# Moving a fetch into the middle of GpSimd's solve, and early parts between stages, in an RWKV-7 and FFN kernel

## The chip, the cores and the metric

The kernel runs on one core of a Trainium2 chip. A core has five engines that run side by side, each with its own queue of instructions taken in order: TensorE (PE, matmuls; its weight loads are listed as PEld), VectorE (DVE), ScalarE (ACT), GpSimd (POOL) and SyncE (SP). They meet through semaphores. Transfers run on 16 DMA engines; SP and GpSimd issue them here, and a transfer that has to wait for something holds up all that stands behind it on the queue that issues it. The metric is the device time of one execution in microseconds (us).

## The reference

First an RWKV-7 recurrence, for 4 batches of 8 heads, 768 steps, head dimension 40. All of it is 32-bit floating point.

```python
for t in range(S):
    kt, vt, rt = (k[:, :, t], v[:, :, t], r[:, :, t])
    wt, at, bt = (w[:, :, t], a[:, :, t], b[:, :, t])
    y[:, :, t] = np.einsum('bhd,bhde->bhe', rt, state)
    Sa = np.einsum('bhde,bhe->bhd', state, at)
    state_decay = state * wt[:, :, None, :] - np.einsum('bhd,bhe->bhde', Sa, bt)
    state = state_decay + np.einsum('bhd,bhe->bhde', vt, kt)
```

Then y, laid out as 3072 tokens of 320 channels, goes through a feed-forward net with a squared ReLU:

```python
h = np.maximum(x @ w_in, 0.0)        # w_in: 320 x 2048
return (h * h @ w_out)               # w_out: 2048 x 320
```

The two weights come as 64-bit numbers and are turned into 32-bit ones by the kernel itself.

## The kernel before

**Chunks.** A recurrence step by step would be 768 steps long, so the sequence is cut into 6 chunks of 128 steps for each of 4 batches: 24 chunks, in the order chunk 0 of every batch, chunk 1 of every batch, and so on. A chunk takes all 8 heads. Within it the recurrence becomes matrix products, with one thing left that is sequential: a strictly triangular 128 x 128 matrix for each head (N, the products of b and a under the decays) must be turned into the inverse of a unit triangular matrix, called T here. T is found for two 64 x 64 halves of each head, and the block between the halves is applied by a product.

**The parts of a chunk.** Each is a Python generator that emits a few instructions to several engines and then yields.

- `early(i)` (L341): loads of w, b and a; transposes of w on TensorE; running products of the decays on VectorE (L351, L352); their two reciprocals (L355, L356); transposes of b and a; bT and aT (L359, L360); the products N on TensorE, copied out by ScalarE (L367 to L372). The decays are stored in HBM (kept_e) for later, and N in blocks (kept_q for the first six chunks, kept_d after them, kept_n for the part between the halves).
- The inverse: `take(u)` (L403, its transfer L412) fetches N of a whole unit of chunks into the tile half_n, one (chunk, head, half) to a partition or two, and `solve(u)` (L414) runs the forward substitution on GpSimd, row by row: at each step s one product (L435) and one subtraction (L437), then the result half_t is stored as kept_t (L440). It is written over by the next unit, whose memset (L425) waits for the store.
- `inverses(i)` (L444): T of one chunk is loaded from kept_t, by SP (L451). For the first six chunks GpSimd has only inverted 32 x 32 blocks (L457 loads them); two rounds of small products, the joins, make the 64 x 64 inverses of them (emitted at L479 and L487, `mm` at L87 is the line that the profile shows).
- `rest(i)` (L494): loads of k, r, v, b (L142) and of the kept decays (L152); the products A, RV; T.
- `chain(i)` (L561): what depends on the state of the chunk before: xr and its products with T, the new state, RX, and the output tokens.
- `ffn()` (L655): for each three chunks of finished tokens, w_in products (ps_f from tokens), squares on VectorE, w_out products.
- `rounding()` (L249): the weights' conversion, in pieces, by ScalarE and VectorE, in stages 0 to 4.

**Units.** GpSimd solves chunks in units: unit 0 holds chunk 0, unit 1 chunk 1, unit 2 chunks 2 and 3, unit 3 chunks 4 and 5, unit 4 chunks 6 and 7, unit 5 chunks 8 and 9, unit 6 chunks 10 to 13, unit 7 chunks 14 to 17, unit 8 chunks 18 to 21, unit 9 chunks 22 and 23. Units 0 to 3 are the fine ones (32 x 32 blocks, 31 steps); the others have 63 steps.

**Stages.** After a prelude (chunks 0 to 3's early parts and units 0 to 2), the main loop has 24 stages, one for each chunk i. A stage weaves, step by step over 12 steps, the chain of chunk i, some steps of `ffn`, the `rest` of chunk i + 1, the early parts of the chunks in `ahead[i]`, and in the first stages pieces of the weights. Nothing reorders what is emitted: each engine runs its queue as the weave wrote it. After each stage, where all chunks of the next unit have had their early parts, the loop emits its fetch and its solve:

```python
ahead = {0: (4, 5), 1: (6, 7), 2: (8,), 3: (9,), 4: (10, 11), 5: (12, 13)}
ahead.update({i: (i + 8,) for i in range(6, len(order) - 8)})
...
while unit < len(units) and all(m_ in done for m_ in range(len(order)) if unit_of[m_] == unit):
    flush()
    take(unit, own)
    solve(unit)
    unit += 1
```

GpSimd has nothing else to do in the main loop, so it runs fetch, solve, store, fetch, solve, store as fast as the chunks' blocks come, far ahead of or behind the stage in which these were emitted. SP's queue holds, in the order of the weave, the loads of `rest` and `early`, the stores of N and the decays, the moves of finished tokens (L108), and the loads of T, each of which waits for its unit's store.

Of the kernel before, what the change touches and what calls it, by code (L numbers as in the profile page):

```python
# [17 lines left out]
def kernel(  # L18
# [22 lines left out]
    nc = tc.nc  # L41
    ctx.enter_context(tc.manual_schedule())
    B, H, S, D = r.shape
    DM = H * D
    DFF = moe_w_in.shape[1]
    C = 128
    MID = C // 2
    HC = C // 2
# [67 lines left out]
    class Ring:  # L116
# [6 lines left out]
        def next(self):  # L123
            self.at = (self.at + 1) % len(self.tiles)
            return self.tiles[self.at]
# [173 lines left out]
    FINE = 4  # L299
# [41 lines left out]
    def early(i, g=None):  # L341

        x_ = early_loaded.pop(i)
        dec = decays.next() if g is None else kept_here[i]
        if g is not None:
            nc.vector.memset(dec[:, :A_, :, MID:MID + 1], 1.0)
        up, down, aT = (dec[:, n] for n in (UP, DOWN, A_))
        wT = turn(x_["w"])
        yield
        for q in range(NP):  # L350
            nc.vector.tensor_tensor_scan(up[:, q, MID + 1:C + 1], wT[:, q, MID:], ones, 1.0, Alu.mult, Alu.mult)  # L351
            nc.vector.tensor_tensor_scan(down[:, q, MID - 1::-1], wT[:, q, MID - 1::-1], ones, 1.0, Alu.mult, Alu.mult)  # L352
        yield
        bT_, aT_ = turn(x_["b"]), turn(x_["a"])
        nc.vector.reciprocal(down[:, :, MID + 1:C + 1], up[:, :, MID + 1:C + 1])  # L355
        nc.vector.reciprocal(up[:, :, :MID], down[:, :, :MID])  # L356
        yield
        bT = turned("bT", 1)
        nc.vector.tensor_tensor(bT, bT_, down[:, :, 1:C + 1], Alu.mult)  # L359
        nc.vector.tensor_tensor(aT[:, :, :C], aT_, up[:, :, :C], Alu.mult)  # L360
        if g is None:
            store(kept_e[i], dec[:USED])
        yield
        bb, c = order[i]
        t_ = new("N", [128, H, C], 1)
        even, odd = products(bT, aT[:, :, :C])
        nc.scalar.copy(t_[:, :NP], even)  # L367

        for half in range(2):
            own_, other = (slice(n * HC, (n + 1) * HC) for n in (half, 1 - half))  # L370
            nc.scalar.copy(t_[own_, NP:, own_], odd[other, :, other])
        nc.scalar.copy(t_[:HC, NP:, HC:], odd[:HC, :, HC:])  # L372
        joins = lambda half: t_[half * HC:half * HC + Q, :, half * HC + Q:(half + 1) * HC]
        for half in range(2):
            for n in range(2):
                at = half * HC + n * Q
                if i < SMALL:
                    kept, to = kept_q[i, :, half, n], at + Q
                else:
                    u = unit_of[i]  # L380
                    kept, to = kept_d[u][i - units[u][0], :, half], (half + 1) * HC
                    kept = kept[:, n * Q * HC:n * Q * HC + Q * (to - at)].rearrange("h (s t) -> h s t", s=Q)
                store(kept.rearrange("h s t -> s h t"), t_[at:at + Q, :, at:to], 1, nc.scalar if g is not None and n else nc.sync)
            if i < SMALL and g is None:
                store(kept_m[i][half], joins(half), 1)
        if g is None:
            store(kept_n[i], t_[:HC, :, HC:], 1)
        else:
            g["dec"], g["N"] = dec, new("N21", [HC, H, HC], 2)
            nc.scalar.copy(g["N"], t_[:HC, :, HC:])  # L390
            g["joins"] = spare("joins", i)
            for half in range(2):
                nc.scalar.copy(g["joins"][half * HC:half * HC + Q], joins(half))
        yield
# [5 lines left out]

    part_of = lambda u: given[:, u % 3 * Q * Q:(u % 3 + 1) * Q * Q] if u < FINE else given

    def take(u, queues):  # L403
        first, nb = units[u]
        if u < FINE:
            kept = kept_q[first:first + nb].rearrange("b h f k s t -> (b h f k) (s t)")
        else:
            kept = kept_d[u].rearrange("b h f w -> (b h f) w")
        cols = classes(u)
        rows = 128 // cols  # L410
        for col in range(cols):
            queues[col % len(queues)].dma_start(out=part_of(u)[col * rows:(col + 1) * rows], in_=kept)  # L412

    def solve(u, between={}):  # L414

        first, nb = units[u]
        fine = u < FINE
        size = Q if fine else HC
        cols = classes(u)
        rows = 128 // cols  # L420
        part = part_of(u)
        words = size // cols * size
        at = u * Q * Q // 2 if fine else 0
        ts = solved[:, at:at + words]
        nc.gpsimd.memset(ts, 0.0)  # L425
        for col in range(cols):
            nc.gpsimd.memset(ts[col * rows:(col + 1) * rows, col::size + cols], -1.0)
        t3 = ts.rearrange("p (j t) -> p j t", t=size)
        for s in range(size - 1):
            if s in between:  # L430
                between[s]()
            n, m_ = s // cols + 1, size - 1 - s
            at = s * size + s + 1 if s < Q else Q * HC + (s - Q) * (Q + 1) + 1
            p_ = new("half_p", [128, 528], 1)[:, :n * m_].rearrange("p (j t) -> p j t", j=n)
            nc.gpsimd.tensor_tensor(p_, part[:, at:at + m_].unsqueeze(1).to_broadcast([128, n, m_]),  # L435
                                    t3[:, :n, s:s + 1].to_broadcast([128, n, m_]), Alu.mult)
            nc.gpsimd.tensor_tensor(t3[:, :n, s + 1:], t3[:, :n, s + 1:], p_, Alu.subtract)  # L437
        to = kept_t[u]
        to = to.rearrange("n b h f k j t -> (n b h f k) (j t)") if fine else to.rearrange("n b h f j t -> (n b h f) (j t)")
        nc.gpsimd.dma_start(out=to, in_=ts)  # L440
# [3 lines left out]
    def inverses(i, g, queue=nc.sync):  # L444
        bb, c = order[i]
        u = unit_of[i]
        kept = kept_t[u][:, i - units[u][0]]
        g["T"] = T = new("T", [128, H, HC], 2)
        if u >= FINE:
            for col in range(classes(u)):  # L450
                queue.dma_start(out=T[col::classes(u)], in_=kept[col].rearrange("h f j t -> (f j) h t"))  # L451
        else:


            blocks = new("blocks", [128, H, Q], 1)
            for col in range(classes(u)):
                queue.dma_start(out=blocks[col::classes(u)], in_=kept[col].rearrange("h f k j t -> (f k j) h t"))  # L457
        if "N" not in g:
            g["N"] = new("N21", [HC, H, HC], 2)
            queue.dma_start(out=g["N"], in_=kept_n[i])  # L460
            if u < FINE:
                g["joins"] = spare("joins", i)
                for half in range(2):
                    queue.dma_start(out=g["joins"][half * HC:half * HC + Q], in_=kept_m[i][half])
        if u >= FINE:
            return
        yield
        upper_ = spare("turned", i)
        nc.vector.transpose(upper_.rearrange("p h t -> p (h t)"), blocks.rearrange("p h t -> p (h t)"))
        for n in range(2):  # L470
            nc.scalar.activation(T[:, :, n * Q:(n + 1) * Q], blocks, Act.Copy, scale=which[:, n:n + 1])
        yield
        small = lambda: psum(ps_w)[:, :H * Q].rearrange("p (h t) -> p h t", h=H)
        p_ = small()
        mv = spare("mv", i)
        ends_ = [(slice(half * HC, half * HC + Q), slice(half * HC + Q, (half + 1) * HC)) for half in range(2)]
        for one, two in ends_:
            for h in range(H):
                mm(p_[two, h], g["joins"][one, h], upper_[one, h], True)  # L479
        for one, two in ends_:  # L480
            nc.scalar.copy(mv[two], p_[two])
        yield
        p_ = small()
        for one, two in ends_:
            for h in range(H):
                mm(p_[one, h], mv[two, h], blocks[two, h], True)
        for one, two in ends_:  # L487
            nc.scalar.copy(T[one, :, Q:], p_[one])
        yield
# [205 lines left out]
    def run(gen):  # L695
        for _ in gen:
            tick()
# [87 lines left out]


    TOTAL = 12
    ahead = {0: (4, 5), 1: (6, 7), 2: (8,), 3: (9,), 4: (10, 11), 5: (12, 13)}
    ahead.update({i: (i + 8,) for i in range(6, len(order) - 8)})

    PER, LAG = NF // 2 + 4 * GB, 3
    by_then = [0] * B + [5]
# [3 lines left out]
    pieces_in = {0: (4, TOTAL), 1: (6, TOTAL), 2: (6, TOTAL), 3: (7, TOTAL), B: (4, 4)}  # L796
    done = set(range(B))
    unit = unit_of[B]
    for i in range(len(order)):
        bb, c = order[i]  # L800
        n, begin = share[i]
# [16 lines left out]
        weave(*jobs)  # L818
        while unit < len(units) and all(m_ in done for m_ in range(len(order)) if unit_of[m_] == unit):
            flush()  # L820
            take(unit, own)
            solve(unit)
            unit += 1
    flush()
    run(second)
# [30 lines left out]
```

## Time and profile before

| | |
|---|---|
| median of 11 runs | 1063.18 us (1061.2 to 1066.32) |
| the profiled execution's own time | 1064.23 us |
| its span | 1062.5 us |
| TensorE busy | 943.4 us, 89% of the span |
| GpSimd busy | 667.1 us, 63% |
| VectorE busy | 497.6 us, 47% |
| ScalarE busy | 273.1 us, 26% |
| granted TensorE clock, mean | 0.90 of full |
| GpSimd idle before L435, for fetched blocks (kept_d) | 59.5 us in 6 waits |
| GpSimd idle before L412, for a unit's blocks to be stored | 36.2 us in 3 waits |
| TensorE idle for T | 16.6 us in 2 waits |

Where GpSimd stood with each unit, in us from the start of the span:

| unit | chunks | fetch issued | first product | result's store issued |
|---|---|---|---|---|
| 3 | 4, 5 | 111.37 | 122.21 | 149.55 |
| 4 | 6, 7 | 157.37 | 173.80 | 250.76 |
| 5 | 8, 9 | 251.36 | 265.81 | 345.23 |
| 6 | 10 to 13 | 346.00 | 356.85 | 478.21 |
| 7 | 14 to 17 | 489.16 | 505.47 | 627.30 |
| 8 | 18 to 21 | 646.52 | 662.98 | 783.88 |
| 9 | 22, 23 | 784.58 | 797.99 | 878.64 |

The stages' first products (A with v) start at 104.43 us for stage 1, 154.28 for stage 2, then 192.76, 231.67, 279.94, 321.77, 356.39, 398.93, 435.57, 469.82 for stage 10, 526.17, 561.95, 597.80, 641.60 for stage 14, 683.21, 720.44, 759.82, 791.16 for stage 18, 835.94, 873.85, 903.85, 935.09 and 971.86 for stage 23.

In a line of the profile's timeline the first number is the start in us, the second the length in us, then engine, line of the kernel, operation, what is written and read, and how many instructions were merged (x16 and the like). A bracket gives the idle time of the engine just before, and what is taken to have ended it: the last event on record, which need not be the true one. A q behind an engine's name is its queue of DMA and semaphore instructions. The row PEclk of the page shows TensorE's granted clock in tenths of full speed.

### The profile page before, as it was taken

How to read it: one execution, taken by the hardware profiler on the slowest of the kernel's cores; microseconds unless marked ns; L12 is line 12 of the kernel's file. 1: busy time of each engine (PE TensorE's matmuls, PEld its weight loads, DVE VectorE, ACT ScalarE, POOL GpSimd, SP SyncE). 2: the span in 40 equal slices, each digit the busy share in tenths (PEclk: the TensorE clock that was granted, in tenths of full speed). 3: DMA queues.
4: the chain of work that ended last, by engine and by line, in shares of the span. 5: the costliest groups of instructions: out<-in, count | busy, mean ns of one | idle time of the engine just before them, and what ended most of it. 6: DMA issues, size and time to landing. Idle time of an engine off the chain costs nothing.

```text
span 1062.5 us, 19797 instructions
## 1 busy us (share of the span) xinstructions
PE 943.4 (89%) x7824; PEld 683.8 (64%) x7824; DVE 497.6 (47%) x940; ACT 273.1 (26%) x627; POOL 667.1 (63%) x1124
## 2 busy tenths in 40 slices
PE   6364668779999999997999998999997999999998
PEld 5264556667677766774677666776675677757656
DVE  5456786697564375251663453363522442222120
ACT  3132332443322223221212222213211222232020
POOL 4778464885888699981899951999958980000000
PEclk8656565578999999998999999899998999999999
DMA  8988989759647916528647618544344431430000
GB/s 106 152 142 147 177 194 176 146 128 181 102 78 140 191 44 93 110 44 177 108 59 135 112 63 140 87 101 77 50 113 95 65 48 53 98 45 7 22 1 19
DMA packets 260168, 106.92 MB, mean 101 GB/s; under 512 B 243660, under 2 KB 249292, under 8 KB 258412
## 3 DMA queue, kind: packets, MB, share of 16 engines
q1 hardware_dynamic: 255740, 86.65, 46.7%
q0 software_dynamic: 3248, 18.88, 7.9%
q8 instruction: 62, 1.02, 0.4%
q10 hardware_dynamic: 1088, 0.13, 0.1%
q14 instruction: 30, 0.25, 0.1%
HBM read 72.47 MB, written 31.19 MB: 98 GB/s over the span
## 4 chain that ended last, share of the span: by engine, by line
PE 56%; POOL 20%; DMA 11%; DVE 5%; issue 4%; ACT 3%; SPq 2%; DVEq 0%; POOLq 0%; ACTq 0%
PE ps_f L87 25%; PE ps_w L87 13%; PE ps_c L87 12%; POOL half_t L437 10%; POOL half_p L435 9%; PE ps_w L314 3%; DMA half_n<-kept_d 2%; DMA in_v<-in_v_dram 2%; DMA dec<-kept_e 2%; DMA kept_e<-decay 1%; DMA kept_t<-half_t 1%; DMA blocks<-kept_t 1%; DVE decay L355 1%; DMA tokens<-tokens 1%; PE ps_c L609 1%
## 5 line engine op out<-in xcount | busy, mean ns | idle before, releaser
L435 POOL TENSOR_TENSOR half_p<-half_n,half_t 128x70 f32<-128x70 f32 (+52 forms) x502 | 296.5, 591 | 110.9 <-DMA half_n<-kept_d 59.5
L437 POOL TENSOR_TENSOR half_t<-half_t,half_p 128x70 f32<-128x70 f32 (+52 forms) x502 | 323.2, 644 | 39.3
L87 PE MATMUL ps_f<-w_out,hid 128*128 128x320 f32 x672 | 202.6, 447 | 0.0
L653 DVE TENSOR_TENSOR hid<-hid 128x384 f32<-128x384 f32 x128 | 93.9, 748 | 143.4 <-ACT hid L671 143.0
L87 PE MATMUL ps_f<-tokens,w_in 128*128 128x384 f32 x448 | 160.9, 503 | 0.0
L87 PEld LDWEIGHTS ps_f<-w_out,hid 128*128 128x128 f32 x672 | 123.6, 193 | 46.5 <-issue 4.7
L87 PEld LDWEIGHTS ps_f<-tokens,w_in 128*128 128x128 f32 x448 | 81.3, 191 | 76.6 <-issue 32.7
L671 ACT ACTIVATE hid<-ps_f 128x384 f32<-128x384 f32 x112 | 54.9, 490 | 199.3 <-PE ps_f L87 199.3
L330 DVE TENSOR_TENSOR A<-ps_w,upper 128x512 f32<-128x512 f32 x48 | 30.9, 686 | 91.3 <-PE ps_w L87 91.3
L506 DVE TENSOR_TENSOR kvT<-ps_w,dec 128x512 f32<-128x512 f32 x24 | 16.5, 688 | 96.9 <-PE ps_w L314 37.2
L87 PE MATMUL ps_c<-xr,T 64*64 64x40 f32 x768 | 40.6, 247 | 23.4 <-DMA T<-kept_t 16.6
L87 PEld LDWEIGHTS ps_c<-xr,T 64*64 64x64 f32 x768 | 33.8, 153 | 35.0 <-issue 18.1
L87 PE MATMUL ps_f<-tokens,w_third 64*128 64x384 f32 x224 | 55.1, 540 | 0.0
L351 DVE TENSOR_TENSOR_SCAN decay<-ps_w,ones 128x64 f32<-128x64 f32 x88 | 23.9, 271 | 65.0 <-PE ps_w L314 65.0
L87 PE MATMUL ps_w<-decay,bT 40*128 40x128 f32 x352 | 30.7, 322 | 24.8 <-DVE decay L360 22.5
L87 PEld LDWEIGHTS ps_w<-decay,bT 40*128 40x128 f32 x352 | 26.0, 221 | 33.5 <-DVE decay L360 18.4
L330 DVE TENSOR_TENSOR RX<-ps_w,upper 128x512 f32<-128x512 f32 x48 | 30.8, 684 | 31.4 <-PE ps_w L87 31.1
L330 DVE TENSOR_TENSOR RV<-ps_w,upper 128x512 f32<-128x512 f32 x48 | 30.9, 686 | 21.5 <-PE ps_w L87 21.2
L87 PE MATMUL ps_w<-rT,xnT 40*128 40x128 f32 x384 | 36.3, 300 | 2.4 <-ACT rT L516 1.9
L355 DVE RECIPROCAL decay<-decay 128x256 f32<-128x256 f32 x22 | 38.3, 1741 | 0.0
L356 DVE RECIPROCAL decay<-decay 128x256 f32<-128x256 f32 x22 | 37.3, 1694 | 0.0
L87 PEld LDWEIGHTS ps_w<-rT,kvT 40*128 40x128 f32 x384 | 27.6, 205 | 14.1 <-issue 4.7
(139 smaller groups left out, 1396.0 us busy)
## 6 DMA issues: line engine op xcount, KB each, us to landing
kept_e<-decay SPq DMA_DIRECT2D x22, 633.8 KB
dec<-kept_e SPq DMA_DIRECT2D x22, 633.8 KB
hid<-in_moe_w_out_dram SPq DMA_DIRECT2D x16, 320.0 KB
half_n<-kept_d POOLq DMA_DIRECT2D x12, 384.0 KB, 11.1
half_n<-kept_d POOLq DMA_DIRECT2D x6, 768.0 KB, 12.2
in_w<-in_w_dram SPq DMA_DIRECT2D x24, 160.0 KB
in_ab<-in_b_dram SPq DMA_DIRECT2D x24, 160.0 KB
in_ab<-in_a_dram SPq DMA_DIRECT2D x24, 160.0 KB
```

Source lines behind the costliest of these rows:

```text
L87: nc.tensor.matmul(o, l_, r_, start=start, stop=True, skip_group_check=True)
L314: nc.tensor.transpose(p_[:, q * 128:(q + 1) * 128], pair(x_, q), ident)
L330: nc.vector.tensor_tensor(t_, p_, over4(upper), Alu.mult)
L351: nc.vector.tensor_tensor_scan(up[:, q, MID + 1:C + 1], wT[:, q, MID:], ones, 1.0, Alu.mult, Alu.mult)
L355: nc.vector.reciprocal(down[:, :, MID + 1:C + 1], up[:, :, MID + 1:C + 1])
L356: nc.vector.reciprocal(up[:, :, :MID], down[:, :, :MID])
L435: nc.gpsimd.tensor_tensor(p_, part[:, at:at + m_].unsqueeze(1).to_broadcast([128, n, m_]), t3[:, :n, s:s + 1].to_broadcast([128, n, m_]), ...
L437: nc.gpsimd.tensor_tensor(t3[:, :n, s + 1:], t3[:, :n, s + 1:], p_, Alu.subtract)
L506: nc.vector.tensor_tensor(kT, kT_, down[:, :, 1:C + 1], Alu.mult)
L609: nc.tensor.transpose(p_[:, q * 128:(q + 1) * 128], pair(xn, q), ident)
L653: nc.vector.tensor_tensor(h_, h_, h_, Alu.mult)
L671: nc.scalar.activation(h_, p_, Act.Relu)
```

## The change

It does four things.

1. A solve can now be cut in two. Unit 4's is: before its step 33, GpSimd issues the fetch of the first 2048 words of each row of unit 5 (all that steps 0 to 31 read), then goes on with unit 4, stores it, and fetches the other 1024 words. Steps 33 and later of unit 4 read only words past those first 2048. The other units are fetched as before.
2. Early parts are dealt out differently: chunk 9 goes from stage 3 to stage 2, chunk 10 from stage 4 to stage 3, chunk 18 from stage 10 to stage 9, and chunks 19 to 23 each one stage sooner (stages 10 to 14; stage 15 has none any more). So unit 5 is complete after stage 2 (stage 3 before), unit 8 after stage 12 (13) and unit 9 after stage 14 (15).
3. The joins of the first six chunks go through the two halves in turn for each head, instead of all heads of one half and then of the other.
4. For chunks 4 to 9 the two reciprocals are emitted one step of the early part sooner, right behind the running products.

```diff
@@ early
             nc.vector.tensor_tensor_scan(down[:, q, MID - 1::-1], wT[:, q, MID - 1::-1], ones, 1.0, Alu.mult, Alu.mult)
+
+        def inverted():
+            nc.vector.reciprocal(down[:, :, MID + 1:C + 1], up[:, :, MID + 1:C + 1])
+            nc.vector.reciprocal(up[:, :, :MID], down[:, :, :MID])
+
+        if B <= i < 10:
+            inverted()
         yield
         bT_, aT_ = turn(x_["b"]), turn(x_["a"])
-        nc.vector.reciprocal(down[:, :, MID + 1:C + 1], up[:, :, MID + 1:C + 1])
-        nc.vector.reciprocal(up[:, :, :MID], down[:, :, :MID])
+        if not B <= i < 10:
+            inverted()
         yield
@@ take and solve
-    def take(u, queues):
+    EARLIER = Q * HC
+
+    def take(u, queues, words=slice(None)):
...
-            queues[col % len(queues)].dma_start(out=part_of(u)[col * rows:(col + 1) * rows], in_=kept)
+            queues[col % len(queues)].dma_start(out=part_of(u)[col * rows:(col + 1) * rows, words], in_=kept[:, words])

     def solve(u, between={}):
+        run(solving(u, between))
+
+    def solving(u, between={}, stop=None):
...
                 between[s]()
+            if s == stop:
+                yield
@@ inverses
-        for one, two in ends_:
-            for h in range(H):
+        for h in range(H):
+            for one, two in ends_:
                 mm(p_[two, h], g["joins"][one, h], upper_[one, h], True)
...
-        for one, two in ends_:
-            for h in range(H):
+        for h in range(H):
+            for one, two in ends_:
                 mm(p_[one, h], mv[two, h], blocks[two, h], True)
@@ the main loop
-    ahead = {0: (4, 5), 1: (6, 7), 2: (8,), 3: (9,), 4: (10, 11), 5: (12, 13)}
-    ahead.update({i: (i + 8,) for i in range(6, len(order) - 8)})
+    ahead = {0: (4, 5), 1: (6, 7), 2: (8, 9), 3: (10,), 4: (11,), 5: (12, 13)}
+    ahead.update({i: (i + 8,) for i in range(6, 9)})
+    ahead[9] = (17, 18)
+    ahead.update({i: (i + 9,) for i in range(10, len(order) - 9)})
...
+    AHEAD, under_way = (FINE,), []
...
             flush()
-            take(unit, own)
-            solve(unit)
+            if under_way:
+
+                take(unit, own, slice(0, EARLIER))
+                run(under_way.pop())
+                take(unit, own, slice(EARLIER, Q * (HC + Q)))
+            else:
+                take(unit, own)
+            if unit in AHEAD:
+                under_way.append(solving(unit, stop=Q + 1))
+                next(under_way[0])
+            else:
+                solve(unit)
             unit += 1
```

Here B is 4, Q is 32, HC is 64 and FINE is 4.

## The prediction

> **What bounds the kernel now.** I read the page's 40 slices first, to see where TensorE is not full, then its chain, then the waits of TensorE and GpSimd, and last the timeline around each hole.
>
> ```profile
> PE   6364668779999999997999998999997999999998
> POOL 4778464885888699981899951999958980000000
> PEclk8656565578999999998999999899998999999999
> ...
> PE 56%; POOL 20%; DMA 11%; DVE 5%; issue 4%; ACT 3%; SPq 2%; DVEq 0%; POOLq 0%; ACTq 0%
> ```
>
> A slice is 26.6 us. Two regimes show. Up to about 235 us TensorE is three to eight tenths busy, mostly near half clock; the stages there are tied together by VectorE, DMAs and in-order waits. From 250 us it is full, except for dents in slices 19, 25 and 31. GpSimd, full almost without a break until 480 us, makes a fifth of the chain. In the full region a TensorE hole costs its own length, so I price those.
>
> The first dent, from the timeline of 462 to 522 us:
>
> ```profile
> 478.21 0.60 POOL L440 DMA_DIRECT2D kept_t<-half_t  x1 [0.30 <-POOL half_t L437]
> 482.44 1.35 SPq L451 DMA_DIRECT2D T<-kept_t  x2
> ...
> 486.01 1.08 PE L87 MATMUL ps_c<-xr,T 64*64 64x40 f32 x16 [9.57 <-DMA T<-kept_t]
> ...
> 488.59 4.21 PE L87 MATMUL ps_f<-tokens,w_in 128*128 128x384 f32 x8
> ...
> 489.16 1.03 POOL L412 DMA_DIRECT2D half_n<-kept_d  x2 [10.35 <-DMA kept_d<-N]
> ```
>
> Unit 6's inverses leave GpSimd at 478.21, SP can load chunk 10's T at 482.44, and TensorE, which had nothing to do from 476.44, starts at 486.01. The bracket is the wait, 9.57 us. It then runs at half clock: w_in x8 took 4.21 (2.85 at full clock elsewhere), w_third x4 1.65 (0.92), the T products 1.08 (0.66), which makes 2.5. First hole: 12.1 us.
>
> The second, from 645 to 682 us:
>
> ```profile
> 646.52 1.03 POOL L412 DMA_DIRECT2D half_n<-kept_d  x2 [18.61 <-DMA kept_d<-N]
> 646.56 0.39 SPq L142 DMA_DIRECT2D in_r<-in_r_dram  x1
> ...
> 663.50 1.09 PE L314 MATMUL ps_w<-ident,in_r 128*128 128x128 f32 x4 [3.34 <-DVE decay L356]
> ...
> 665.74 2.82 PE L87 MATMUL ps_w<-rT,xnT 40*128 40x128 f32 x16
> ```
>
> The releaser named (a reciprocal) is not what I believe: the r load was issued at 646.56, 0.04 us after GpSimd began its fetch for unit 8, and would land near 663.4, 17 us later. The fetch had waited 18.61 us for chunk 21's blocks. Cost: 3.34 waiting, then half clock: two transposes at 1.09 for about 0.63, rT products 2.82 for 1.16, w_out x8 4.28 for 2.42, so 4.4. Second hole: 7.7 us.
>
> The third, from 776 to 828 us:
>
> ```profile
> 783.88 0.60 POOL L440 DMA_DIRECT2D kept_t<-half_t  x1 [0.30 <-POOL half_t L437]
> 784.58 1.95 POOL L412 DMA_DIRECT2D half_n<-kept_d  x4
> ...
> 786.66 12.71 SPq L108 DMA_DIRECT2D tokens<-tokens  x8
> ...
> 799.48 1.37 SPq L451 DMA_DIRECT2D T<-kept_t  x2
> ...
> 803.15 1.08 PE L87 MATMUL ps_c<-xr,T 64*64 64x40 f32 x16 [7.08 <-DMA T<-kept_t]
> ...
> 804.16 4.63 PE L87 MATMUL ps_f<-w_out,hid 128*128 128x320 f32 x8
> ```
>
> Unit 8 ends at 783.88. Its T for chunk 18 stands on SP behind eight token copies, which here take 12.71 us (6.3 to 6.4 in stages 8, 11 and 14), because the fetch of unit 9 runs beside them. Cost: 7.08, plus 0.4 and 2.2 at half clock. Third hole: 9.7 us. The three make 29.5 us.
>
> **What the Trainium skill says.** "DMA: Bandwidth & Descriptors", section "Queues, rings and completion order": a DMA engine takes queues in turn, a packet at a time, so loads on SP slow down beside GpSimd's fetch; the 17 us of the r load agrees. The same page, "Anatomy of one DMA": the wait of a DMA on a semaphore is on the issuing sequencer; GpSimd's 18.61 us idle before a fetch agrees, so a fetch placed in mid-unit can stop the unit. "TensorE: Matmul & The Clock Gate", "HAM oscillation": idle gaps over some 3.4 us drop the clock to half; here 9.57, 7.08 and already 3.34 did. "TensorEngine Tiling", "Instruction Overhead": some 60 cycles for each matmul; the joins' records come every 53 ns at half clock (32 in 1.70), which is 64 cycles, so overlap between row groups can save little.
>
> **The change, part by part.**
>
> Joins. The same 32-record groups, in another order. Bounds: 0, by the overhead above; up to 0.6 us a group, by the 1.08 against 1.38 us that 16 records took with alternating row groups and with one. Six chunks, two groups: 12 x 0.3 = 3.6, about half while TensorE is what the stage waits for: -2 us.
>
> Reciprocals. The pair costs 1.74 + 1.70 wherever it stands. Moved ahead of RX, RV and weight pieces, it delays those by 3.4 and bT comes no sooner where VectorE is busy throughout: in stage 1 it runs from 132 to 148 us without a gap. For chunk 5 bT could come 3.4 sooner (TensorE waited 10.28 for it), but its N copy still waits until 100.58 for chunk 4's N to be stored. So 0, at most 3 either way.
>
> Early parts. Chunk 9 moves from stage 3 to stage 2, 10 from 4 to 3, 11 takes stage 4; chunk 18 moves to stage 9, and 19 to 23 go one stage sooner. Each brings two loads of a and b, one of w, a kept_e store and five stores of N on SP. Stage 1, with two early parts, lasts 49.9 us (first product of A at 104.43, next at 154.28); stage 2, with one, 38.5. Of the 11.4, six weight pieces at five operations of 0.68 instead of 0.49 explain 5.7. So stage 2 grows by 5.7 to 11.4; I take 8. Stage 4 sheds one: between its TensorE records at full clock (0.6 + 1.1 + 1.2 = 2.9) and the 7.2 between stages 5 and 6 (41.8, 34.6); I take 4. Chunk 18 puts 2.9 ahead of chunk 10's T, taken out again later; chunk 18's own stores come to stand behind that T on SP, where only unit 8, at 608, asks for them.
>
> The mid-unit fetch. It stands before step 33 of unit 4, 214.9 us in the trace before. It waits for chunk 9's blocks. With stage 2 at 46 us, chunk 9's products come near 200, its copies and the stores behind the token copies near 205, landed about 210: no wait, 5 us to spare. Behind it stand 30 steps of unit 4 (36 us), then units 5 and 6. Four more issues cost 4 x 0.49 = 1.95 on GpSimd. It meets the loads of stage 3: 0 to 4, I take 2. What it removes is here, in the timeline before:
>
> ```profile
> 250.76 0.60 POOL L440 DMA_DIRECT2D kept_t<-half_t  x1 [0.30 <-DMA in_w<-in_w_dram]
> 251.36 1.94 POOL L412 DMA_DIRECT2D half_n<-kept_d  x4
> ...
> 257.48 0.96 POOL L425 MEMSET half_t<- 128x1024 f32 x1 [4.18 <-DMA kept_t<-half_t]
> ...
> 265.81 0.29 POOL L435 TENSOR_TENSOR half_p<-half_n,half_t 128x63 f32<-128x63 f32 x1 [6.72 <-DMA half_n<-kept_d]
> ```
>
> Unit 5's first product waits until 265.81 for data; with two thirds of the words landed and the rest not needed before step 32, it waits only for unit 4's store and the memset, so 6.7 less, and up to 1.9 more since that store shares with a third of the fetch. Net of 1.95: 4.8 to 6.7, I take 5.5, which passes through unit 6, as chunk 13's blocks (bT at 319) are ready well before 346.
>
> Sum up to the first hole. TensorE arrives at 476.4 + 8 + 2 - 4 - 2 + 2.9 = 483.3. Chunk 10's T: 486.0 - 5.5, plus 1.5 because unit 7's fetch, no longer waiting 10.35 for chunk 17 (whose stores now stand ahead of that T on SP), runs beside it: 482.0. The wait is gone and the clock stays up: -12.1, against +4 lost early.
>
> Later. Unit 7 starts some 18 us sooner and ends near 608. Chunk 21's blocks come in stage 12, so unit 8's fetch goes out then, mid-stage, far from the loads of stage 14: -7.7. Unit 8 ends near 743, and chunk 18 wants its T near 774: -9.7. Unit 7's fetch now meets stage 10's loads and unit 9's those of stage 17, which have 17 and 23 us before they are used, not 13.5 as in stage 14: I leave 3 for both.
>
> Total: -12.1 - 7.7 - 9.7 + 4 + 3 = -22.5. The profiled execution's own time is 1064.2 (span 1062.5, 1.7 around it), so 1041.7; it stands 1.05 above the median of the runs, 1063.2, and I say 1041.
>
> **The rivals.** (a) The early stages eat the gain at the first hole: stages 2 and 3 grow by 20 in all instead of 10, or the T comes late; then 10 us are lost again: 1051, between 1047 and 1058. For it: one collision already costs SP 8.78 us at 158.3. Against it: the weight pieces are narrower there. (b) Slower: the mid-unit fetch waits W us for chunk 9's blocks, at 215 us. TensorE then waits 482 + W - 483.3 at chunk 10, with half clock after it, and the end is about 1041.7 + W: slower than before from W about 23. In the trace before chunk 9's blocks were issued from 229.45 to 231.8, landing near 236, which is W = 21: if the earlier place brings chunk 9 forward by nothing, it decides. Against it: its stores now follow stage 2's end, near 201, where before they followed that of stage 3, at 231.7. At W = 30, 1071. (c) Nothing: the early loss grows to 26 and balances all: 1063. (d) Early stages lose nothing and the joins give their 3.6: under 1033.
>
> **How the numbers follow.** Forecast (1033 to 1047) 0.60, (a) 0.22, (b) 0.09, (c) 0.04, (d) 0.05. 1033 to 1057 leaves out (d), (b), (c) and the tail of (a), 2 in 10. A measurement tells 0.2% (2.1 us) from no change. Faster 0.86, same 0.05, slower 0.09.
>
> **What would show it.** Right: no wait for chunk 10's T, or under 3 us; unit 5's first product within 9 us of unit 4's store; fetches of units 7 and 8 with no idle before them; no dents in slices 25 and 31. Wrong: GpSimd idle before the mid-unit fetch; stage 2 over 52 us; new waits for r or k loads in stages 10 or 17; half clock around 480.

## The result, and the profile after

The changed kernel takes 1055.13 us (median of 13 runs, 1048.7 to 1059.95) against 1063.62 us for the kernel before on the same chips; the ratio is 0.9914, with a 95% interval of 0.9898 to 0.9929. It is faster by 8.5 us, where 22 were forecast. (Every ratio here is to the kernel before as it ran beside the run in question; its median differs a little from one to the next.) The profiled execution took 1057.01 us with a span of 1055.3, that is 7.2 us both below the one of before, and the accounts below are made between these two.

The page of the changed kernel: its slices (26.4 us each) and the chain.

```profile
PE   6355775687999799999999999999999999999998
POOL 4778464897898499993999957999758830000000
PEclk8657555657999899999999999999999999999999
...
PE 76%; DMA 9%; DVE 4%; ACT 4%; issue 2%; POOL 2%; SPq 2%; DVEq 0%; ACTq 0%; POOLq 0%
```

The dents in slices 19, 25 and 31 are gone, from 370 us on the clock is full, and GpSimd's share of the chain fell from 20% to 2%. But the early region is longer, and there is one new dent, in slice 14. The first product of A in each stage shows where the time went, in us (length of the stage; the first row is the start of stage 1):

| | before | after | difference | forecast |
|---|---|---|---|---|
| up to stage 1 | 104.4 | 105.6 | +1.2 | -2 for all joins |
| stage 2 | 38.5 | 49.4 | +10.9 | +8 |
| stage 3 | 38.9 | 39.3 | +0.4 | +2 |
| stage 4 | 48.3 | 47.6 | -0.7 | -4 |
| stage 6 | 34.6 | 44.2 | +9.6 | none |
| stage 9 | 34.3 | 36.5 | +2.3 | +2.9 |
| stage 10, first hole | 56.4 | 43.8 | -12.5 | -12.1 |
| stage 14, second hole | 41.6 | 34.3 | -7.3 | -7.7 |
| stage 15 | 37.2 | 35.2 | -2.1 | -2.9 |
| stage 18, third hole | 44.8 | 35.6 | -9.2 | -9.7 |
| all other stages | | | +0.2 | +3 |

The three holes close by what was forecast, each within half a microsecond. What was lost ahead of them, with stage 15's part taken out again, is 21.8 us (23.9 less 2.1) instead of 4.

The first and the third hole's place, from the timeline of the changed kernel:

```profile
479.05 0.60 POOL L455 DMA_DIRECT2D kept_t<-half_t  x1 [0.30 <-DMA in_ab<-in_b_dram]
486.30 2.12 SPq L466 DMA_DIRECT2D T<-kept_t  x2
487.59 1.03 POOL L422 DMA_DIRECT2D half_n<-kept_d  x2 [7.94 <-DMA kept_d<-N]
500.44 0.66 PE L87 MATMUL ps_c<-xr,T 64*64 64x40 f32 x16
...
798.55 0.66 PE L87 MATMUL ps_c<-xr,T 64*64 64x40 f32 x16 [0.51 <-ACT xr L599]
```

Chunk 10's T products no longer wait, but they stand at 500.44, not at 483; and unit 6 ends at 479.05, no sooner than before (478.21). Nor was T there at 482: the last update of its load's semaphore in the trace is at 498.55, 1.9 us before TensorE came for it. (Where TensorE does wait for T, its products start 0.14 us after that update: 485.87 and 486.01 before the change.) So this hole did not close because T came in time, but because TensorE came still later. Chunk 18's products have no wait for T and run at full clock (0.66 against 1.08).

The two places that grew. Stage 2, timeline of the changed kernel:

```profile
158.90 1.95 POOL L422 DMA_DIRECT2D half_n<-kept_d  x4 [7.66 <-DMA kept_d<-N]
160.17 13.41 SPq L142 DMA_DIRECT2D in_b<-in_b_dram  x1
173.63 0.88 SPq L142 DMA_DIRECT2D in_w<-in_w_dram  x1
178.92 1.09 PE L314 MATMUL ps_w<-ident,in_w 128*128 128x128 f32 x4 [8.18 <-DMA in_w<-in_w_dram]
```

GpSimd sends unit 4's fetch out at 158.90. SP's next load takes 13.41 us to issue (8.78 before), so that chunk 9's w is asked for at 173.63, and TensorE, in order, stands 8.18 us before it with stage 2's own products behind. Before the change this w was wanted a stage later. Then the same two loads stood almost in the same place, and the products that read w had no wait:

```profile
158.32 8.78 SPq L142 DMA_DIRECT2D in_b<-in_b_dram  x1
...
172.73 1.01 SPq L142 DMA_DIRECT2D in_w<-in_w_dram  x1
...
196.32 1.06 PE L314 MATMUL ps_w<-ident,in_w 128*128 128x128 f32 x4
```

Stage 6, timeline of the changed kernel:

```profile
340.12 0.57 SPq L142 DMA_DIRECT2D in_k<-in_k_dram  x1
...
341.40 0.40 SPq L142 DMA_DIRECT2D in_r<-in_r_dram  x1
...
342.37 1.03 POOL L422 DMA_DIRECT2D half_n<-kept_d  x2
342.51 9.16 SPq L142 DMA_DIRECT2D in_b<-in_b_dram  x1
...
358.56 0.28 POOL L450 TENSOR_TENSOR half_p<-half_n,half_t 128x63 f32<-128x63 f32 x1 [6.51 <-DMA half_n<-kept_d]
...
358.76 1.09 PE L314 MATMUL ps_w<-ident,in_r 128*128 128x128 f32 x4 [5.00 <-DMA in_r<-in_r_dram]
...
363.38 4.17 PE L87 MATMUL ps_f<-w_out,hid 128*128 128x320 f32 x8
```

Before the change, the load of r was issued 17 us ahead of the fetch:

```profile
329.05 0.40 SPq L142 DMA_DIRECT2D in_r<-in_r_dram  x1
...
346.00 1.03 POOL L412 DMA_DIRECT2D half_n<-kept_d  x2 [0.16 <-issue]
```

Now TensorE is 12 us later here than before, GpSimd 3.6 us sooner, and so stage 6's loads and unit 6's fetch go out within 2.5 us of each other. Both suffer: TensorE waits 5.00 us for r and drops to half clock (4.17 for 2.42), and unit 6's first product comes at 358.56, where it came at 356.85 before. The 3.6 us by which GpSimd was ahead were lost at the very next fetch.

### The profile page after: what moved, and what is told of

The parts are those of the page before. It is cut to its first block, busy times and chain, and to the rows that moved or that the text cites. A ratio compares the mean times of both kernels' runs of the same rounds, so it can differ in the third digit from the quotient of the medians.

```text
span 1055.3 us, 19794 instructions
## 1 busy us (share of the span) xinstructions
PE 937.0 (89%) x7824; PEld 678.6 (64%) x7824; DVE 500.1 (47%) x940; ACT 273.6 (26%) x627; POOL 671.0 (64%) x1128
## 4 chain that ended last, share of the span: by engine, by line
PE 76%; DMA 9%; DVE 4%; ACT 4%; issue 2%; POOL 2%; SPq 2%; DVEq 0%; ACTq 0%; POOLq 0%
PE ps_f L87 37%; PE ps_c L87 16%; PE ps_w L87 15%; PE ps_w L314 5%; DMA blocks<-kept_t 2%; DMA in_r<-in_r_dram 2%; SPq L108 1%; PE ps_w L549 1%; DMA in_w<-in_w_dram 1%; DMA in_v<-in_v_dram 1%; PE ps_c L624 1%; POOL half_t L452 1%; POOL half_p L450 1%; PE ps_c L559 1%; DMA dec<-kept_e 1%
## 5 line engine op out<-in xcount | busy, mean ns | idle before, releaser
L452 POOL TENSOR_TENSOR half_t<-half_t,half_p 128x70 f32<-128x70 f32 (+52 forms) x502 | 324.6, 647 | 39.3
L87 PE MATMUL ps_f<-w_out,hid 128*128 128x320 f32 x672 | 200.3, 443 | 0.0
L330 DVE TENSOR_TENSOR RV<-ps_w,upper 128x512 f32<-128x512 f32 x48 | 30.9, 686 | 19.5 <-PE ps_w L87 19.2
L87 PE MATMUL ps_c<-RX,in_b 128*64 128x128 f32 x384 | 30.3, 298 | 8.0 <-DVE RX L330 8.0
```

Of the source, the lines that this page charges most:

```text
L87: nc.tensor.matmul(o, l_, r_, start=start, stop=True, skip_group_check=True)
L330: nc.vector.tensor_tensor(t_, p_, over4(upper), Alu.mult)
```

## The experiments

The theory: each fetch of a unit slows whatever SP issues beside it. The new order put three such pairs together (unit 4's fetch with chunk 9's loads in stage 2; unit 6's with stage 6's loads; unit 7's with chunk 10's T), and the late dealing alone closes the second and third hole. The rivals: the early loss is VectorE's work or SP's order, and the holes closed only because TensorE came later.

**e1: unit 6's fetch moved off stage 6's loads.**

```diff
+                if unit == 6:
+                    for _ in range(18):
+                        nc.gpsimd.memset(new("half_p", [128, 528], 1), 0.0)
                 take(unit, own)
```

> The changed kernel with 18 memsets of half_p (about 8 us of GpSimd work, results unused) between unit 5's store and unit 6's fetch. Theory (stage 6's hole comes from unit 6's fetch at 342.4 going out within 2.5 us of stage 6's own loads): the loads land before the fetch, TensorE's 5.0 us wait for the r load and the half clock after it go, stage 6 takes 35 to 37 us instead of 44.2, unit 6 ends only 2 to 5 us later because its memset waits until 349.8 anyway, and the time is 1045 to 1050. Rival (the loads are late by themselves, since SP issues them behind five stores of N at 335 to 340): stage 6 keeps its 44 us and the time is 1054 to 1060.

Measured: 1056.44 us, ratio 0.9939 (0.9918 to 0.9961). From the timeline of this run:

```profile
352.44 1.02 POOL L422 DMA_DIRECT2D half_n<-kept_d  x2 [0.17 <-DMA in_ab<-in_a_dram]
353.44 0.60 PE L314 MATMUL ps_w<-ident,in_r 128*128 128x128 f32 x4
...
484.43 0.60 POOL L455 DMA_DIRECT2D kept_t<-half_t  x1 [0.30 <-POOL half_t L452]
498.69 1.08 PE L87 MATMUL ps_c<-xr,T 64*64 64x40 f32 x16 [6.45 <-DMA T<-kept_t]
```

The r load is no longer waited for, and stage 6 takes 37.5 us instead of 44.2: 6.7 of the 9.6 us of growth are the collision. But the time did not follow: TensorE, 8 us sooner at chunk 10, waits there 6.45 us for T, whose products start 14.3 us after unit 6's store (7.8 before the change). By the semaphore T lands at 498.55 here, as it did in the changed kernel. TensorE's arrival moved from 500.4 to 492.2 us, but T's did not move, and all that TensorE could gain was the 1.8 us between 500.44 and 498.69.

**e2: without the mid-unit fetch.**

```diff
-    AHEAD, under_way = (FINE,), []
+    AHEAD, under_way = (), []
```

> The changed kernel without the mid-unit fetch: unit 5 fetches after unit 4's store, as before the change; all else stays. Theory (the mid-unit fetch's 3.6 us pulled unit 6's fetch onto stage 6's loads, so it cost more than it gave): unit 6's fetch goes out near 346, most of the loads have landed, stage 6 takes 35 to 39 us, unit 6 ends at 479 to 481, chunk 10's T comes at about 487 and TensorE waits 2 to 5 us for it: 1047 to 1052. Rival (the mid-unit fetch is a gain of 5 us that is still in the time): 1058 to 1061.

Measured: 1056.6 us, 0.9931 (0.9908 to 0.9955), not to be told from the changed kernel (its profiled execution, span 1051.6, is the quickest of five). Stage 6 takes 34.7 us, unit 6 stores at 479.74 and the T products come 15.1 us later. So within the change as made, the mid-unit fetch moved unit 6's end by 0.7 us between these two executions, or by some 3.6 if one counts that GpSimd was 2.9 us ahead in this one already at unit 3's store (147.70 for 150.63). The theory had the places right and the T's landing too early by 6 us; the rival's gain of 5 us is not there in the time.

**e3: the early dealing of before, the late one of after.**

```diff
-    ahead = {0: (4, 5), 1: (6, 7), 2: (8, 9), 3: (10,), 4: (11,), 5: (12, 13)}
+    ahead = {0: (4, 5), 1: (6, 7), 2: (8,), 3: (9,), 4: (10, 11), 5: (12, 13)}
...
-    AHEAD, under_way = (FINE,), []
+    AHEAD, under_way = (), []
```

> The changed kernel with the early parts of stages 2 to 4 dealt as before the change (8; 9; 10 and 11) and no mid-unit fetch; chunk 18 in stage 9 and 19 to 23 one stage sooner stay, and so do the joins and the reciprocals. Theory (the early loss comes from chunk 9 in stage 2, and the two late holes close by the late dealing alone): stage 5 begins at 280 to 282 (279.9 before, 291.9 after), no hole in stage 6, the wait for chunk 10's T is back at 6 to 9 us, no waits at the places of the second and third hole: 1043 to 1048. Rival (the late holes closed only because TensorE ran 11 us later there): one or both are back, 1053 to 1062.

Measured: 1050.84 us, 0.9893 (0.9857 to 0.9928). Stage 5 begins at 276.9 us (after: 291.9), stage 6 takes 35.2, stages 14 and 18 take 34.1 and 35.6 us, as in the changed kernel. So the loss up to stage 5 is the early dealing's (e2, which keeps that dealing, keeps stage 2's 50.3 us), and the late holes close by the late dealing alone, whenever TensorE gets there. What was missed: the wait for chunk 10's T is 15.0 us, not 6 to 9, because its products now start 13.9 us after unit 6's store:

```profile
477.36 0.60 POOL L455 DMA_DIRECT2D kept_t<-half_t  x1 [0.30 <-POOL half_t L452]
...
491.25 1.08 PE L87 MATMUL ps_c<-xr,T 64*64 64x40 f32 x16 [15.02 <-DMA T<-kept_t]
```

So with TensorE on time the first hole is open, and wider than before the change.

**e4: the reciprocals back where they were.**

```diff
-        if B <= i < 10:
-            inverted()
         yield
         bT_, aT_ = turn(x_["b"]), turn(x_["a"])
-        if not B <= i < 10:
-            inverted()
+        inverted()
```

> The changed kernel with the reciprocals of chunks 4 to 9 back behind the transposes of b and a. Theory (stage 2's 10.9 us have two parts, 8.2 of waiting for chunk 9's in_w and 3.6 of waiting for RX behind chunk 9's reciprocals): stage 2 takes 45 to 47 us instead of 49.4, the rest as it was: 1050 to 1054, unless stage 6's hole changes by as much. Rival (VectorE has the same work in stage 2 wherever the pair stands): stage 2 at 49 to 50, 1054 to 1057; or bT comes later and N with it, 1057 to 1060.

Measured: 1049.68 us, 0.9879 (0.9851 to 0.9908), better than the changed kernel by 5.4 us in the medians and by 3.7 in the ratios, whose intervals still touch; but not where the theory said: stage 2 still takes 49.3 us, so the wait for RX there costs nothing of its own. Stage 3 takes 34.9 instead of 39.3, and stage 6 34.2 instead of 44.2. In this run stage 3's loads of w, b and a go out from 213.7 to 217.8 us and in the changed kernel from 218.4 to 228.4, behind the mid-unit fetch of 215.8; and TensorE is 6 us sooner at stage 5, so that stage 6's loads of k, r and v are issued from 334.4 to 336.1, ahead of unit 6's fetch at 340.44. That the reciprocals moved SP's loads by way of the weight pieces on VectorE, which stand ahead of them, is argued from the order on SP, not shown.

**e5: unit 7's fetch moved off chunk 10's T**, in the kernel of e3:

```diff
+                if unit == 7:
+                    for _ in range(18):
+                        nc.gpsimd.memset(new("half_p", [128, 528], 1), 0.0)
                 take(unit, own)
```

> The kernel of e3 (old dealing of stages 2 to 4, no mid-unit fetch) with 18 memsets of half_p (11 us of GpSimd work, results unused) between unit 6's store and unit 7's fetch. Theory (chunk 10's T lands 14 us after unit 6's store instead of 7.8, because unit 7's fetch now runs beside it): the T products start 8 us after the store, near 485.5 instead of 491.25, nothing later changes: 5 to 6.5 us off the time of e3, 1044 to 1047. Rival (the T is late because of SP's own queue or of the reads' length): still 14 us after the store, 1049 to 1053.

Measured: 1057.1 us, 0.9947 (0.9929 to 0.9966). Timeline of this run:

```profile
475.41 0.60 POOL L455 DMA_DIRECT2D kept_t<-half_t  x1 [0.30 <-POOL half_t L452]
483.43 1.08 PE L87 MATMUL ps_c<-xr,T 64*64 64x40 f32 x16 [3.80 <-DMA T<-kept_t]
486.93 1.02 POOL L422 DMA_DIRECT2D half_n<-kept_d  x2 [0.22 <-DMA kept_d<-N]
488.15 0.57 SPq L142 DMA_DIRECT2D in_k<-in_k_dram  x1
...
498.87 1.08 PE L314 MATMUL ps_w<-ident,in_k 128*128 128x128 f32 x4 [8.11 <-DMA in_k<-in_k_dram]
```

The T products start 8.0 us after the store instead of 13.9: the fetch beside T is what costs 6 us. But then the fetch meets stage 10's k load, TensorE waits 8.11 us for that, and stage 10 takes 61.1 us as it did with the fetch on T. "Nothing later changes" fell: the fetch costs about the same on whichever of the two it falls, and by the ratios the kernel is some 6 us slower than without the memsets. Where these 6 us lie is not shown: the profiled execution is the quickest of the seven.

**e6: the mid-unit fetch later**, under the early dealing of before; against the changed kernel:

```diff
-    ahead = {0: (4, 5), 1: (6, 7), 2: (8, 9), 3: (10,), 4: (11,), 5: (12, 13)}
+    ahead = {0: (4, 5), 1: (6, 7), 2: (8,), 3: (9,), 4: (10, 11), 5: (12, 13)}
...
-                under_way.append(solving(unit, stop=Q + 1))
+                under_way.append(solving(unit, stop=Q + 20))
```

> The kernel of e3 with the mid-unit fetch, placed before step 52 of unit 4 (near 240 us, after chunk 9's blocks have landed under the old dealing) instead of step 33. Theory (the mid-unit fetch makes unit 5 some 5 us sooner, which reaches chunk 10's T if no load of stage 6 meets unit 6's fetch): unit 6 stores at 471 to 474 instead of 477.4, T products at 486 to 488, 1045 to 1048. Rival (unit 6's fetch, 4 us sooner, gives it back): unit 6 stores at 476 to 479, 1049 to 1054.

Measured: 1046.46 us, 0.9842 (0.9816 to 0.9867), with e10 the best here, ahead of the changed kernel by 8.7 us and of the one before by 17. Timeline of this run:

```profile
240.38 2.00 POOL L422 DMA_DIRECT2D half_n<-kept_d  x4
...
340.29 1.03 POOL L422 DMA_DIRECT2D half_n<-kept_d  x2 [0.17 <-DMA in_ab<-in_a_dram]
...
351.91 0.29 POOL L450 TENSOR_TENSOR half_p<-half_n,half_t 128x63 f32<-128x63 f32 x1 [6.85 <-DMA half_n<-kept_d]
473.22 0.60 POOL L455 DMA_DIRECT2D kept_t<-half_t  x1 [0.30 <-POOL half_t L452]
487.76 1.08 PE L87 MATMUL ps_c<-xr,T 64*64 64x40 f32 x16 [6.81 <-DMA T<-kept_t]
```

As the theory had it: there is no wait ahead of the mid-unit fetch, unit 6's first product comes 11.6 us after its fetch (16.2 in the changed kernel), its store at 473.22 (477.36 in e3, without the mid-unit fetch), and the time falls by 4.4 us (by 5.4 in the ratios). How much of unit 6's 4.1 us is the mid-unit fetch is less sure: unit 3's store was 3.8 us sooner in this execution, and e5 and e10, which are the same kernels as e3 and e6 up to here, store at 475.41 and 474.03. That makes 1.4 to 4.1 us of the 5.5 that the prediction gave it, if nothing meets the fetch after it.

**e7: the late dealing alone**, on the kernel before:

```diff
-    ahead.update({i: (i + 8,) for i in range(6, len(order) - 8)})
+    ahead.update({i: (i + 8,) for i in range(6, 9)})
+    ahead[9] = (17, 18)
+    ahead.update({i: (i + 9,) for i in range(10, len(order) - 9)})
```

> The kernel before with one part of the change alone: chunk 18's early part in stage 9 and those of 19 to 23 one stage sooner. Theory (the late dealing closes the second and third hole alone; joins and reciprocals give nothing): like e3, 1047 to 1053. If the earlier reciprocals cost what e4 gave back (4 to 6 us in the stages up to 5), this kernel is 3 to 5 us faster than e3 unless GpSimd's T hides it. Rival (the late holes need the other parts): 1055 to 1063.

Measured: 1051.54 us, 0.9889 (0.9868 to 0.9910), the same as with joins and reciprocals changed as well (0.9893). So the late half of the second part of the change is worth 12 us alone, and all the rest together took some 3 of it back (0.9914 to 0.9889, intervals that overlap). But e6 shows that the rest can give 5 when it is placed otherwise.

**e8: chunk 9's loads first on SP** in stage 2:

```diff
+        if i == 2:
+            load_early(9)
         if i + 1 < len(order):
```

> The changed kernel with the loads of w, b and a of chunk 9 issued at the head of stage 2, ahead of the k, dec, r, v and b loads of stage 2 on SP. Theory (stage 2 is long because in_w of chunk 9 stands on SP behind an in_b whose issue takes 13.4 us beside unit 4's fetch): TensorE's 8.2 us wait for in_w goes, stage 2 takes 41 to 45 us instead of 49.4, stage 5 begins 4 to 8 us sooner; the time follows by 0 to 5 us only, since chunk 10's T then sets the end: 1050 to 1055. Rival (the wait moves to the loads that now stand behind): stage 2 at 48 to 51, 1054 to 1058.

Measured: 1055.45 us, 0.9926 (0.9897 to 0.9956). The rival: stage 2 takes 53.0 us, even more than it said. The wait for w is gone, and TensorE waits for the stage's k, which now stands behind, beside the same fetch:

```profile
172.69 1.12 PE L314 MATMUL ps_w<-ident,in_k 128*128 128x128 f32 x4 [13.18 <-DMA in_k<-in_k_dram]
```

**e9: unit 4's fetch behind stage 2's loads.** The memsets of e1, 36 of them and for unit 4:

```diff
+                if unit == 4:
+                    for _ in range(36):
+                        nc.gpsimd.memset(new("half_p", [128, 528], 1), 0.0)
                 take(unit, own)
```

> The changed kernel with 36 memsets of half_p (21 us of GpSimd work, results unused) between unit 3's store and unit 4's fetch, which moves that fetch from 159 to about 172 us, behind stage 2's loads, and the mid-unit fetch from 216 to about 229. Theory (stage 2 is 10.9 us longer because chunk 9's early part needs, in the same stage, loads that land only with unit 4's fetch; stage 3 loses 4 us because the mid-unit fetch meets its loads): stage 2 takes 42 to 45 us, what remains over 38.5 being VectorE's work; stage 3 takes 34 to 36. Units 4 to 6 run 13 us later and so does chunk 10's T: 1057 to 1066, which is not the question here. Rival (stage 2 is long because of VectorE's second early part and the order on TensorE): stage 2 takes 48 to 50.

Measured: 1053.7 us, 0.9904 (0.9877 to 0.9931). Timeline of this run:

```profile
160.96 4.82 SPq L142 DMA_DIRECT2D in_b<-in_b_dram  x1
...
173.69 1.96 POOL L422 DMA_DIRECT2D half_n<-kept_d  x4
```

Stage 2 falls from 49.4 to 40.7 us, with the same work on VectorE and TensorE and the same order on SP: 8.7 of its 10.9 us of growth are the fetch. At most 2.2 are work, and perhaps none: under the old dealing the stage took from 36.7 to 42.1 us in the seven other runs that had it. Stage 3 did not follow (40.7): its loads are issued 9 us after the stage's start and waited for 5.5 us without any fetch near, so the fetch is not all that makes them late. And units 4 to 6 store 6 to 12 us later than in the changed kernel, at no cost in the time that can be told.

**e10: unit 7's fetch between T and the next loads.** The kernel of e6 with 8 memsets ahead of unit 7's fetch:

```diff
+                if unit == 7:
+                    for _ in range(8):
+                        nc.gpsimd.memset(new("half_p", [128, 528], 1), 0.0)
                 take(unit, own)
```

> The kernel of e6 with 8 memsets of half_p (about 5 us) between unit 6's store and unit 7's fetch, so that the fetch begins just as chunk 10's T has landed and before the next loads of stage 10 are issued. Theory (the T lands 14.5 us after the store only because of the fetch beside it): the T products start 8 to 10 us after the store, TensorE's 6.8 us wait shrinks to under 3, stage 10 takes 46 to 49 us instead of 53.3: 1039 to 1043. Rival (what the T gains, stage 10's own k load loses, as in e5): stage 10 at 52 to 56, 1045 to 1049.

Measured: 1045.78 us, 0.9824 (0.9804 to 0.9845), which cannot be told from 0.9842. The T products come 9.8 us after the store, but 3.6 us of wait for k, and the half clock behind it, take the place of what T gained: the rival again.

**e11: the reciprocals back** in the kernel of e6; the edit is that of e4.

> The kernel of e6 with the reciprocals of chunks 4 to 9 back behind the transposes of b and a. Theory (in e4 the reciprocals were worth 5 us only because stage 3's loads, 4 us earlier, came clear of the mid-unit fetch at 216, and stage 6's of unit 6's fetch; in e6 neither meets): no difference from e6, 1044 to 1049. Rival (the earlier reciprocals cost VectorE time in stages 0 to 3 by themselves): 1039 to 1043.

Measured: 1052.13 us, 0.9870 (0.9840 to 0.9899): neither range. It is slower than e6 by 3.0 us in the ratios, with intervals that overlap (the two ran on different chips), and by 4.9 than e10, which ran beside it. Unit 6 stores 2.9 us later than in e6 (476.15), which is what stage 11 starts later by (530.62, 527.58), but 2.2 of these were there at unit 3's store; stage 15 takes 2.2 more. So the same edit gained on the changed kernel and gains nothing here: it has no price of its own. That it acts by moving transfers on or off each other is what e4's trace suggests; it is not shown.

**e12: the joins alone**, on the kernel before:

```diff
-        for one, two in ends_:
-            for h in range(H):
+        for h in range(H):
+            for one, two in ends_:
                 mm(p_[two, h], g["joins"][one, h], upper_[one, h], True)
```

(and the second group likewise)

> The kernel before with the alternating joins alone. By the forecast: the 32-record groups shrink by 0.3 us each and the time by 2 us, 1061. Rival (the groups are not what the early stages wait for): the groups shrink, the time stays within 1 us of before, 1062 to 1064.

Measured: 1065.66 us, ratio 1.0008 (0.9996 to 1.0021). The groups of the kernel before, and then of this run, by form in the window of 80 to 245 us (busy us, then mean ns of one, then idle before):

```profile
L87 PE MATMUL ps_w<-blocks,hid 32*32 32x32 f32 x128 | 6.3, 226 | 5.9 <-ACT hid L481 5.9
L87 PE MATMUL ps_w<-hid 32*32 32x32 f32 x128 | 6.3, 226 | 0.0
```

```profile
L87 PE MATMUL ps_w<-blocks,hid 32*32 32x32 f32 x128 | 5.0, 227 | 9.9 <-ACT hid L481 9.5
L87 PE MATMUL ps_w<-hid 32*32 32x32 f32 x128 | 3.9, 226 | 0.0
```

Busy time falls from 12.6 to 8.9 us over eight groups, 0.46 each, and the wait ahead of the second group grows by 4.0. TensorE does the joins faster and waits for ScalarE's copies instead, in this window by as much as it saves.

## Why the prediction was wrong, step by step

**Where the miss lies.** The forecast had chunk 10's T products at 483.3 us and the span's end at 1040.0 (1041.7 less the 1.7 around the span), which is 556.7 us later. Measured were 500.44 and 1055.3, 554.8 us later. So the whole miss was made ahead of these products. In e1 to e4 and e6 to e8, too, the span ends 555.7 to 557.3 us after they start, and they start anywhere from 487.76 to 500.62. (In e9 and e11 it is 559.5 and 559.2; in e5 and e10, with the wait for k behind them, 567.8 and 563.4.) They start at the later of two arrivals, TensorE's and T's, and the forecast had both wrong.

**TensorE's arrival, forecast at 483.3.** It was 500.4. Of the terms of that sum:

- **Stage 6** (nothing): +9.6, the largest error, and the step that failed most plainly: "I take 5.5, which passes through unit 6, as chunk 13's blocks (bT at 319) are ready well before 346". The blocks were ready; but the prediction looked only for what the fetch would wait for, not for what would be issued beside it, though it had moved TensorE 4 us later and GpSimd 5.5 us sooner, towards each other.
- **Stage 2** (+8, taken as weight pieces on VectorE): 10.9, and for another reason. The prediction saw SP's 8.78 us beside unit 4's fetch and used it as evidence for rival (a) only; it did not ask which of the moved loads would now be issued beside that fetch and needed in the same stage. Moving the fetch gives back 8.7.
- **Stage 4** (-4): 0.7. Shedding an early part gave nearly nothing; what the stage waits for instead was not looked into. **Joins** (-2): nothing, measured alone. **Reciprocals** (0, at most 3 either way): 0 between e7 and e3 (there with the joins), but 3.7 or 5.4 us, by ratios or medians, in e4; the bound of 3 counted their own length on VectorE and nothing else. **Stage 3** (+2): 0.4 net; the stage takes 34.9 and 36.2 us in two runs, without the early reciprocals and without the mid-unit fetch.

**T's arrival, forecast at 482.0.** T landed at 498.55, 16.6 us later. Unit 6's store was to come 5.5 us sooner and came 0.8 later. Then T's load went out 7.3 us after the store (4.2 before), with chunk 17's stores of N ahead of it on SP (issued from 477.96 to 485.2), and it landed 19.5 us after the store, where the prediction had 7.8 and 1.5 more for sharing with unit 7's fetch. The 1.5 is the step that failed here. In the eight runs in which that fetch follows the store at once, the T products start 13.7 to 15.1 us after the store; it is 7.8 before the change and 8.0 with the fetch held back (e5), so the fetch beside T costs 6 to 7. Hence a repair of TensorE's side alone gains little, which is what e1 found.

**The three holes** (-29.5): 29.0 measured. The second and the third went by the causes named. For the second the profile's releaser (a reciprocal) was set aside for the r load beside unit 8's fetch; with that fetch out of stage 14 the hole went, in every run with the late dealing. Unit 7's and unit 9's fetches had 3 us set aside for them and cost nothing where the change put them. That the first hole's -12.5 agrees with the forecast's -12.1 is luck: it closed because TensorE came 17 us late, and it is open again in each run where TensorE comes sooner (15.0 us of wait in e3, 6.8 in e6).

**No wait before the mid-unit fetch**, and 5 us of gain from it: the first is right; the second only in part, and only under the old early dealing (1.4 to 4.1 us at unit 6's end).

What came true is rival (a), "the early stages eat the gain", at 1055 inside its 1047 to 1058; its mechanism named stages 2 and 3 or a late T. It was stages 2 and 6, and a late T.

None of the signs listed for a wrong forecast appeared. There was no idle time before the mid-unit fetch, stage 2's 49.4 us stayed under the 52 set as a mark, no load of r or k was waited for in stages 10 and 17, and half clock came at 363 and not at 480. Of the signs listed for a right one a single one failed: unit 7's fetch still stood 7.94 us for chunk 17's blocks, so that unit 7 stored at 620.68 and not near 608, at no cost. The signs stood only at the places that the prediction had thought of.

The Trainium skill, "DMA: Bandwidth & Descriptors", section "Queues, rings and completion order", says that a DMA engine drains a whole packet from one queue before it turns to the next. The packets in the traces show what that means here, and more. The changed kernel from 168 to 171 us, with unit 4's fetch (queue q0) beside SP's loads (q1), b's among them:

```profile
q0 software_dynamic: 72, 0.60, 93.4%
q1 hardware_dynamic: 74, 0.01, 3.4%
```

These are packets, MB, and their share of the engines' time. The queues do take turns, one packet each; but a packet of the fetch holds 8.3 KB on average and one of a load 160 bytes, so the fetch gets nearly all of the bandwidth while it lasts. And e6 from 480 to 484 us, with unit 7's fetch beside chunk 10's T, whose load SP had begun to issue at 478.03; the view has a line for each queue that moved anything:

```profile
q0 software_dynamic: 81, 0.80, 94.4%
```

Here SP's queue moves nothing at all for 4 us, and the first packets of T's load come at 484, as the fetch ends. Turns by the packet do not explain that, and no run here shows what does.

## What to carry to other kernels

When a change moves a bulk transfer, or moves one engine against another, list for each such transfer what other queues will issue within its landing time (here 10 to 15 us), and who waits for that in order; a transfer that is never late itself can make what is issued beside it late. Where two chains meet (TensorE and GpSimd at chunk 10), work out the arrival of both, as a gain on one shows only down to the other. When you list the signs of being wrong, add one for the sum (here: the start of chunk 10's T products) and not only signs for the causes you have thought of. Of the parts of a bundled change price each alone: here the late dealing was worth 12 us, and the rest added nothing to it as it was placed.

## What was not expected of the hardware

SP's instruction that issues a load stands still beside a fetch: the same in_b load took 4.82 us to issue with the fetch later, 8.78 before and 13.41 in the changed kernel, and everything behind it on SP waits as long. In the joins, alternating between the halves lets records of 32x32 overlap more: 256 of them with a mean of 226 ns cover 12.6 us before and 8.9 with the new order, the mean unchanged, which is 49 and 35 ns for each. The prediction had read the 53 ns at which they came as a limit of their issue, and it was not one.
